# One kernel on one Trainium2 core: the first row tiles in one transfer, the first weights ahead of the filter's second piece, and 200 places of the order list

## Chip, core and metric

One NeuronCore of a Trainium2 chip runs the whole program. The metric is the device time of one execution in microseconds (us). Three runs of the kernel before gave 195.13, 194.25 and 196.08 us; the median, 195.13, is the time before.

## What is computed

The input `x` (2048 rows of 512, bf16) is normalized row by row. Two branches use the result `xn`: a state-space branch (a short convolution of `k`, times `v`, then a long convolution along the rows with a filter `ssm_k`, times `xn`), and a gated feed-forward branch (512 to 1792 to 512). Cut to what matters:

```python
xn = layernorm(x)                                   # x = A_q
kv = shift_conv(k, shift_k, taps=4) * v
y  = irfft(rfft(kv, 2S) * rfft(ssm_k, 2S))[:S]      # long convolution, S = 2048
s  = xn * (y + kv * ssm_D)
g  = silu((gelu(xn @ w_gate) * (xn @ w_up)) @ w_down)
out = x + s * g
```

## The kernel before, in words

**Tiling.** Row `16p + t` of `x` is partition `p` of row tile `t`, so 16 row tiles of 128x512. The feed-forward branch takes them in four groups `q` of four. In a group, each of 14 units `m` multiplies the transposed `xn` by a block of `Wg` and of `Wu` (four matmuls each, line 618 is the helper that records every plain matmul), ACT applies Gelu into `GE`, DVE multiplies into `HT`; then the `down` matmuls with `Wd` follow.

**The filter.** `ssm_k` comes as four pieces of 128x2048 into `Hn`. Pieces 0 and 1 are transposed on PE (`h_transpose`, lines 870 to 888, the matmuls of L878) into `HTr`; pieces 2 and 3 are rearranged on ACT into `HP` and transposed by DMA into `HTD`. A first Fourier step on PE with the table `F1` then makes eight tiles `AH0` to `AH7` from `HTr` ("H" tiles) and eight, `AJ0` to `AJ7`, from `HTD` ("J" tiles), in `stage1_h` (line 929). Each is evicted from PSUM into one of four places in SBUF and stored from there to the DRAM scratch `ZH`: an H tile by a DMA that ACT issues, a J tile by one that SP issues. `AH4` to `AH7` are made in two halves (`half1`, line 919, rows `X<-psall 128x4x128`), one for each filter piece, so such a tile holds its place from the first half until its store has landed.

**Places that are shared.** The four places of the H tiles are parts of `X` that are not loaded yet, and two of the four places of the J tiles are the same memory (line 485):

```python
ast = {"H": [quarter(X, j) for j in (8, 10, 12, 14)],
       "J": [quarter(T, j) for T, j in ((X, 12), (X, 14), (G, 4), (G, 6))], ...}
```

So J place 0 is H place 2, and J place 1 is H place 3. Each place has a semaphore that its stores raise, `d_astH0` to `d_astH3` and `d_astJ0` to `d_astJ3`. The recorder (`Trk.op`, line 195) makes an instruction wait for the stores of exactly the memory that it overwrites.

**What sets the order.** A planner (`Sched.run`, line 345) walks the list of task numbers `SEQ` in its written order and hands each task to its engine, so `SEQ` alone sets the order of each engine's instructions. From costs in a table the planner also works out times for every task; these decide nothing but which buffer or PSUM bank a tile gets (`Pool_.find`, line 250: the place that came free first; of places free equally long, the first). A tile gets its place when the list comes to the first eviction that writes it. For the first loads the planner is told when they land (`LANDS`, line 304).

**Start.** SP issues the loads one after the other (`load`, line 594, all recorded at L590). PE multiplies zeros 11 times to pass the time (`warm_up`, from the tile `AST`), then transposes filter piece 0, and so on as the list says. DVE takes the statistics of each row tile (L821, L822), POOL the reciprocal root (L831, L832), DVE writes `XN` (L835), PE transposes it (L854), and ACT or DVE evicts it to `xnT` (L609, L612).

Of the kernel before, what the change touches and what calls it, by code (L numbers as in the profile page):

```python
# [22 lines left out]
LAST = [(0, 384), (384, 512)]  # L23
TURN = 8192
N_WARM = 11
ORDER = "x02 h0 h1 x22 w0 w1 h2 h3 D0 w2 s0 k0 v0 x1 w3 k1 v1 d0 d1 k2 v2 k3 v3 x2 x3"
SEQ = (
# [22 lines left out]
)  # L50
NF_BANKS = 4
ISSUE = 470.0
LOAD_NS = {("x0_", 262144): 1400.0, ("x0_", 131072): 450.0, 262144: 900.0, 524288: 1350.0, ("x", 524288): 2100.0, ("h", 524288): 1300.0, ("wg", 524288): 1550.0, ("wu", 524288): 1450.0, 917504: 2620.0, ("sk", 524288): 1500.0, 344064: 1250.0, 46080: 350.0, 3072: 100.0, 1024: 200.0}
W_XT, W_SW, W_BK, W_BH, W_ZI, W_BI, W_ZK, W_MI, W_G1 = 1665000, 600000, 555000, 703000, 333000, 640000, 490000, 740000, 222000
NC_PAIRS = 4
SMALL = 1.15 * 262144
# [235 lines left out]
class Sched:  # L292
# [8 lines left out]
    FIRST = {"loads": 1050.0, "SP": 30500.0}  # L301
    DRAIN = 121.0
    EARLY, TAKEN, SHARED, WAIT = (0.0, 1.0), 1400.0, 46000.0, 3300.0
    LANDS = (4350.0, 5590.0, 7100.0, 8420.0, 9350.0, 10200.0, 11500.0)

    def __init__(self):
        self.tasks = []
# [37 lines left out]
    def run(self):  # L345
        free = dict(self.FIRST)
        pipe = 0.0
        n_loads = 0
        order = []
        pmode = 0  # L350
        for name in SEQ.split():
            t = self.tasks[int(name.rstrip("b"))]
            eng, dur = t.opts[name[-1] == "b"]
            base = 0.0
            for d in t.deps:
                base = max(base, d.end if eng == d.eng == "PE" else d.end + d.lat + (self.SEM if not d.nbytes or eng != "PE" else 400.0 if d.eng == "loads" else self.HEDGE))
            for b in t.w:
                if b.pool is not None and b.slot is None:
                    f, b.slot = b.pool.find()
                    b.pool.take(b.slot)  # L360
                    base = max(base, f + self.SEM)
            t.start, t.eng = max(base, free.get(eng, 800.0)), eng
            free[eng] = t.end = t.start + dur + (self.DRAIN if eng == "PE" and t.mode != pmode else 0.0)
            pmode = t.mode if eng == "PE" else pmode
            if eng == "loads":
                free[eng] = t.start + dur * (self.EARLY[1] if t.start < self.EARLY[0] else 1.0)
                if n_loads < len(self.LANDS):
                    free[eng] = self.LANDS[n_loads] - self.LOAD_LAT
                n_loads += 1
                t.end = free[eng] + self.LOAD_LAT  # L370
            elif t.nbytes:
                en = t.end
                if en < self.SHARED:
                    free["loads"] += self.TAKEN
                pipe = max(pipe, en + self.DMA_LAT / 2) + t.nbytes / (self.SHARE_BW if en < self.SHARED else self.DMA_BW)
                t.end = pipe + self.DMA_LAT / 2 + (self.WAIT if en < self.SHARED else 0.0)
            for b in set(t.r + t.w):
                b.left -= 1
                b.last_end = max(b.last_end, t.end + t.lat)
                if b.left == 0 and b.pool is not None:  # L380
                    b.pool.release(b.slot, b.last_end)
            order.append(t)
        assert sorted(t.n for t in order) == list(range(len(self.tasks)))
        return order
# [14 lines left out]
def build_kernel(nc, A_q, A_k, A_v, A_shift_k, A_ssm_k, A_ssm_D, B_w_gate, B_w_up, B_w_down, out):  # L399
    with ExitStack() as es0:  # L400
# [107 lines left out]
        def dsem(name):  # L508
            return DSem(nc.alloc_semaphore(name), name)
# [79 lines left out]
        def dma(eng, out_ap, in_ap, sem, r, w):  # L589
            trk.dma(eng, lambda e: e.dma_start(out=out_ap, in_=in_ap), sem, r=r, w=w)  # L590
# [3 lines left out]
        def load(name, out_ap, in_ap, w_res, w_buf, nbytes, ring="SP", r=(), rb=()):  # L594
            sem = dsem("d_" + name)
            ns = LOAD_NS.get((name.rstrip("0123456789"), nbytes)) or LOAD_NS[nbytes]
            last_load[0] = S.add([("loads", ns)], lambda e: dma(ring, out_ap, in_ap, sem, r, w_res), r=rb, w=w_buf, nbytes=nbytes)
# [211 lines left out]

        for what in ORDER.split():  # L810
            if what[0] in "xa" and len(what) == 3:
# [475 lines left out]
```

## Time and profile before

| | |
|---|---|
| Runs | 195.13, 194.25, 196.08 us |
| Span of the profiled execution (first to last instruction) | 193.3 us |
| Median of the runs minus that span | 1.8 us |
| Busy: PE, DVE, ACT, POOL | 188.6, 160.0, 125.4, 13.9 us |
| Mean granted TensorE clock | 1.00 |
| DMA | 49.19 MB, mean 254 GB/s |

The profiled execution is one of its own; its span leaves out what lies ahead of the first instruction and behind the last. Sums in the prediction are made in the time of that span, and the 1.8 us are added at the end. In the views a row names line, engine, operation, `out<-in` and a count; in square brackets stands the idle time of the engine just before, and what ended it. "SPq" and "ACTq" are the issues of DMAs. Matmul rows overlap: a 128x512 matmul has a duration of 379 ns in the views, while the next one starts 216 ns after it.

### The profile page before, as it was taken

What the parts mean: (1) busy time and instruction counts of PE and PEld (TensorE: products, weight loads), DVE (VectorE), ACT (ScalarE), POOL (GpSimd) and SP (SyncE); (2) the same over time, 40 slices, a digit from 0 to 9 for tenths busy, and PEclk for the clock granted to TensorE, in tenths of its full rate; (3) what the DMA queues carried; (4) which work ended last, traced back from release to release, by engine and by line L of the source; (5) the groups of instructions that cost most, each with busy time, mean ns of one, the idle gap of its engine ahead of it and who ended that gap; (6) DMA issues with size and microseconds to landing.
All of it is one profiled execution on the core that took longest, in us unless ns stands there. A gap on an engine that the chain in (4) does not pass through costs nothing.

```text
span 193.3 us, 3502 instructions
## 1 busy us (share of the span) xinstructions
PE 188.6 (98%) x1377; PEld 85.6 (44%) x1377; DVE 160.0 (83%) x245; ACT 125.4 (65%) x170; POOL 13.9 (7%) x32
## 2 busy tenths in 40 slices
PE   7899999999999999999999999999999999999993
PEld 2685544444444444443434433433444334444452
DVE  6699789998999995877888789878897863588993
ACT  6787999969885987868548766856577431232121
POOL 5412420000000000020300000000000000000000
PEclk9999999999999999999999999999999999999999
DMA  5999999999999679999999991984805345939333
GB/s 175 311 307 349 377 400 347 157 249 372 375 374 354 196 264 259 390 323 305 218 285 230 338 320 59 288 276 147 264 10 195 106 140 153 389 112 353 132 139 136
DMA packets 45958, 49.19 MB, mean 254 GB/s; under 512 B 12787, under 2 KB 39671, under 8 KB 45942
## 3 DMA queue, kind: packets, MB, share of 16 engines
q1 hardware_dynamic: 37366, 42.67, 70.1%
q10 hardware_dynamic: 8576, 6.29, 10.3%
q8 instruction: 11, 0.18, 0.4%
q14 instruction: 5, 0.04, 0.1%
HBM read 27.39 MB, written 14.68 MB: 218 GB/s over the span
## 4 chain that ended last, share of the span: by engine, by line
PE 93%; DMA 4%; SPq 1%; DVE 1%; ACT 0%; issue 0%
PE psall L618 86%; PE psall L1028 5%; DMA Hn<-in_A_ssm_k_dram 4%; PE psall L854 1%; SPq L590 1%; PE psall L878 1%; DVE G L1175 0%; DVE G L1174 0%; ACT G L1172 0%
## 5 line engine op out<-in xcount | busy, mean ns | idle before, releaser
L618 PE MATMUL psall<-xnT,Wu 128*128 128x512 bf16 (+1 forms) x232 | 55.8, 372 | 0.0
L618 PE MATMUL psall<-xnT,Wg 128*128 128x512 bf16 (+1 forms) x232 | 55.3, 372 | 0.0
L618 PE MATMUL psall<-Wd,HT 128*128 128x512 bf16 (+2 forms) x238 | 52.0, 367 | 0.0
L1140 DVE TENSOR_TENSOR HT<-psall,GE 128x512 bf16<-128x512 f32 x54 | 36.7, 685 | 15.8 <-PE psall L618 15.4
L1137 ACT ACTIVATE GE<-psall 128x512 bf16<-128x512 f32 x54 | 31.7, 601 | 13.1 <-PE psall L618 12.9
L618 PEld LDWEIGHTS psall<-Wd,HT 128*128 128x128 bf16 x238 | 22.4, 98 | 25.9 <-issue 1.1
L618 PEld LDWEIGHTS psall<-xnT,Wg 128*128 128x128 bf16 x232 | 21.9, 98 | 25.4 <-issue 1.3
L618 PEld LDWEIGHTS psall<-xnT,Wu 128*128 128x128 bf16 x232 | 21.6, 98 | 25.9 <-issue 3.5
L609 ACT ACTIVATE X<-psall 128x1024 bf16<-128x1024 f32 (+1 forms) x18 | 15.1, 843 | 3.3 <-DMA ZH<-X 1.9
L609 ACT ACTIVATE HS<-psall 128x1024 bf16<-128x1024 f32 x14 | 13.7, 1022 | 4.4 <-PE psall L1028 4.4
L1164 ACT ACTIVATE G<-psall 128x512 bf16<-128x512 f32 x12 | 7.0, 598 | 12.9 <-PE psall L618 12.4
L1011 DVE TENSOR_TENSOR KAC<-KAC,KTM 128x2048 bf16<-128x2048 bf16 x12 | 14.6, 1217 | 0.1
L1009 DVE TENSOR_TENSOR KTM<-KK,SKB 128x2048 bf16<-128x2048 bf16 x12 | 14.6, 1217 | 0.0
L609 ACT ACTIVATE BO<-psall 128x1024 bf16<-128x1024 f32 x9 | 9.1, 1022 | 8.2 <-PE psall L1028 7.7
L609 ACT ACTIVATE KB<-psall 128x1024 bf16<-128x1024 f32 x11 | 11.0, 1021 | 3.6 <-PE psall L1028 3.6
L609 ACT ACTIVATE AST<-psall 128x1024 bf16<-128x1024 f32 x12 | 12.4, 1033 | 0.7 <-PE psall L618 0.5
L612 DVE CAST BO<-psall 128x1024 bf16<-128x1024 f32 x7 | 8.5, 1224 | 3.7 <-PE psall L1028 3.7
L821 DVE BATCH_NORM_STATS2 stats<-X 128x6 f32<-128x512 bf16 x16 | 10.3, 675 | 1.1 <-DMA X<-in_A_q_dram 1.1
L1172 ACT ACTIVATE G<-psall 128x512 bf16<-128x512 f32 (+2 forms) x5 | 2.6, 512 | 13.1 <-PE psall L618 13.1
L1091 DVE TENSOR_TENSOR HW<-KB,HW 128x1024 bf16<-128x1024 bf16 x16 | 10.9, 682 | 0.0
L1091 DVE TENSOR_TENSOR HS<-KB,HS 128x1024 bf16<-128x1024 bf16 x16 | 10.8, 682 | 0.0
L1166 DVE SCALAR_TENSOR_TENSOR G<-G,psall 128x512 bf16<-128x512 bf16 x12 | 7.8, 680 | 2.0 <-ACT G L1164 2.0
(83 smaller groups left out, 175.6 us busy)
## 6 DMA issues: line engine op xcount, KB each, us to landing
BH<-ZH SPq DMA_DIRECT2D x8, 512.0 KB, 6.1
HW<-HS SPq DMA_DIRECT2D x16, 256.0 KB, 3.2
BK<-ZK SPq DMA_DIRECT2D x8, 512.0 KB, 5.1
ZI<-BO ACTq DMA_DIRECT2D x16, 256.0 KB, 2.8
BI<-ZI SPq DMA_DIRECT2D x8, 512.0 KB, 4.2
ZK<-AST SPq DMA_DIRECT2D x6, 512.0 KB, 4.1
Hn<-in_A_ssm_k_dram SPq DMA_DIRECT2D x4, 512.0 KB, 8.4
KK<-in_A_k_dram SPq DMA_DIRECT2D x4, 512.0 KB, 8.6
```

The lines of the kernel that those rows point to most:

```text
L609: return h.activation(o, i, ACTF.Copy, scale=scale)
L612: return h.tensor_copy(o, i)
L618: return h.matmul(o, lhsT=l, rhs=r, start=st, stop=sp)
L821: t_stats[t] = op([("DVE", 670.0)], lambda e, h, t=t: h.bn_stats(stats[:, t, :], X[:, t, :]), r=[bX[q][t % 4]], w=[bst[t]], rr=[R_X[t]], w ...
L1009: op([("DVE", dur)], lambda e, h, j=j, m=m: h.tensor_tensor(KTM[:, m.slot, :, :], kk(j), sk(j), ALU.mult), r=need + [bSKB[j], a], w=[m], r ...
L1011: op([("DVE", dur)], lambda e, h, m=m: h.tensor_tensor(KAC[:, a.slot, :, :], KAC[:, a.slot, :, :], KTM[:, m.slot, :, :], ALU.add), r=[m], ...
L1028: trk.op("PE", lambda h: h.matmul(ps(s, i)[b, :], lhsT=wt(col)[a, :], rhs=data(col)[a, :], start=n < 16, stop=n >= len(todo) - 16, tile_po ...
L1091: return hd.tensor_tensor(o, flat(KB, kb[h]), o, ALU.mult)
L1137: op([("ACT", act(512))], lambda e, h: h.activation(GE[:, g.slot, :], bank(pg), ACTF.Gelu_apprx_tanh), r=[pg], w=[g], rr=lambda: R_bank(pg ...
L1140: op([("DVE", dve(512, 1))], lambda e, h: h.tensor_tensor(HT[:, q % 2, m, :], bank(pu), GE[:, g.slot, :], ALU.mult), r=[pu, g], w=[bHT[q][m]],
L1164: op([("ACT", act(n))], lambda e, h, g=g, pc=pc: h.activation(g, pc(), ACTF.Tanh, scale=0.5), r=[p], w=[bt], rr=lambda p=p: R_bank(p), ww= ...
L1166: op([("DVE", dve(512, 1))], lambda e, h, g=g, pc=pc: h.scalar_tensor_tensor(out=g, in0=g, scalar=1.0, in1=pc(), op0=ALU.add, op1=ALU.mult ...
```

## The change

It has three parts. Row tiles 0 to 3 come in one transfer of 512 KB in place of two of 256 KB (`x04` for `x02` and `x22` in `ORDER`); there is one load task less, so every later task has a number lower by one. The first blocks of `Wg` and `Wu` (`w0`, in the list their loads) are issued ahead of filter piece 1 (`h1`). And the first 200 or so places of `SEQ` are written anew; behind them the two lists agree but for the numbers. `LANDS` is now given by bytes loaded and not by load. The diff, with `SEQ` cut to the rows that are rewritten:

```diff
-ORDER = "x02 h0 h1 x22 w0 w1 h2 h3 D0 w2 s0 k0 v0 x1 w3 k1 v1 d0 d1 k2 v2 k3 v3 x2 x3"
+ORDER = "x04 h0 w0 h1 w1 h2 h3 D0 w2 s0 k0 v0 x1 w3 k1 v1 d0 d1 k2 v2 k3 v3 x2 x3"
 SEQ = (
-    "17 18 0 3 1 2 4 8 5 7 11 20 6 9 50 12 65 66 67 73 19 68 75 74 49 10 76 13 52 21 82 22 86 117 83 69 107 70 71 112 54 72 87 77 56b 78 53 369 "
-    "51 108 36 79 371 109 84 88 80 370 15 85 372 23 31 89 110 378 377 113 27 373 379 381 383 375 14 453 455 457 380 24 458 374 459 25 454 118 382 "
-    "119 55 456 460 32 120 376 389 102 384 397 399 28 30 33 461 34 29 37 63 38 111 385 387 393 16 59 463 386 103 462 388 464 391 398 104 26 400 "
-    "390 395 105 465 146 394 405 396 99 147 121 466 148 468 150 407 57 409 100 401 403 46 392 402 406 149 151 470 35 404 152 39 96 413 408 469 "
-    "410 472 153 467 411 101 415 473 412 421 154 414 416 58 471 155 422 417 61 423 424 106 429 156 97 114 158 93 60 62 431 44 425 426 427 428 115 "
+    "0 17 18 1 3 8 2 19 20 21 4 11 12 5 6 7 35 9 10 13 66 22 30 26 49 23 24 64 31 67 27 51 74 68 48 65 72 69 75 82 86 76 50 70 106 111 29 101 73 "
+    "81 116 102 71 78 77 83 53 107 85b 376 378 79 14 52 84 88b 87 458 377 369 452 379 456 112 380 382 368 370 371 117 453 55 32 459 372 374 15 "
+    "388 381 454 383 455 33 54 62 373 28 375 384 457 390 392 394 36 37 113 103 393 104 105 386 16 25 45 118 56 119 389 391 396 460 464 461 398 "
+    "145 412 400 395 462 108 148 147 465 114 385 146 149 109 397 110 463 469 58 402 466 387 404 399 413 420 414 470 408 422 150 415 410 405 467 "
+    "34 151 152 153 98 99 57 421 423 120 401 403 38 409 411 60 471 468 472 100 59 61 406 154 155 407 424 426 43 428 157 95 416 417 430 425 427 "
...
-LOAD_NS = {("x0_", 262144): 1400.0, ...
+LOAD_NS = {("x0_", 524288): 1400.0, ...
-    LANDS = (4350.0, 5590.0, 7100.0, 8420.0, 9350.0, 10200.0, 11500.0)
+    LANDS = ((0.0, 2650.0), (524288.0, 4050.0), (1048576.0, 5450.0), (1310720.0, 6320.0), (1572864.0, 7190.0), (2097152.0, 8590.0), (2621440.0, 10590.0), (3145728.0, 12390.0))
...
-                if n_loads < len(self.LANDS):
-                    free[eng] = self.LANDS[n_loads] - self.LOAD_LAT
-                n_loads += 1
+                n_loads += t.nbytes
+                for (b0, t0), (b1, t1) in zip(self.LANDS, self.LANDS[1:]):
+                    if b0 < n_loads <= b1:
+                        free[eng] = t0 + (t1 - t0) * (n_loads - b0) / (b1 - b0) - self.LOAD_LAT
```

Line numbers above 300 are higher by two in the changed kernel: L618 is L620 there, L609 is L611.

**The order at three places.** SP's first issues, before:

```order
L590 DMA X<-in_A_q_dram 128x1024
L590 DMA Hn<-in_A_ssm_k_dram 128x2048
L590 DMA X<-in_A_q_dram 128x1024
L590 DMA Hn<-in_A_ssm_k_dram 128x2048
L590 DMA Wg<-in_B_w_gate_dram 128x4x256
L590 DMA Wu<-in_B_w_up_dram 128x4x256
L590 DMA X<-in_A_q_dram 128x2048
```

and now (the last row is the load of row tiles 4 to 7 in both):

```order
L592 DMA X<-in_A_q_dram 128x2048
L592 DMA Hn<-in_A_ssm_k_dram 128x2048
L592 DMA Wg<-in_B_w_gate_dram 128x4x256
L592 DMA Wu<-in_B_w_up_dram 128x4x256
L592 DMA Hn<-in_A_ssm_k_dram 128x2048
L592 DMA X<-in_A_q_dram 128x2048
```

The second piece of the filter moved from the fourth place to the fifth, and 2.0 MB in place of 1.5 MB have been asked for when it has.

PE after the multiplications by zero, up to the second piece of the filter, with the semaphores that a row waits for (`d_h0` and `d_h1` are the landings of the filter's pieces, `d_wg0` that of the first block of `Wg`). Before:

```order
L878 MATMUL psall<-ident_63,Hn 128x128 [waits d_h0,s_POOL]
L878 MATMUL psall<-ident_63,Hn 128x128 x7
L854 MATMUL psall<-ident,XN 128x128 [waits s_DVE]
L854 MATMUL psall<-ident,XN 128x128 x3
L618 MATMUL psall<-HTr,F_58 128x256 [waits s_ACT]
L618 MATMUL psall<-HTr,F_58 128x256
L854 MATMUL psall<-ident,XN 128x128 [waits s_DVE]
L854 MATMUL psall<-ident,XN 128x128 x3
L618 MATMUL psall<-HTr,F_58 128x256 x4
L878 MATMUL psall<-ident_63,Hn 128x128 [waits d_h1]
```

and now:

```order
L880 MATMUL psall<-ident_63,Hn 128x128 [waits d_h0,s_POOL]
L880 MATMUL psall<-ident_63,Hn 128x128 x7
L856 MATMUL psall<-ident,XN 128x128 [waits s_DVE]
L856 MATMUL psall<-ident,XN 128x128 x3
L620 MATMUL psall<-HTr,F_58 128x256 [waits s_ACT]
L620 MATMUL psall<-HTr,F_58 128x256 x5
L856 MATMUL psall<-ident,XN 128x128 [waits s_DVE]
L856 MATMUL psall<-ident,XN 128x128 x3
L620 MATMUL psall<-HTr,F_58 128x256 x2
L856 MATMUL psall<-ident,XN 128x128 [waits s_DVE]
L856 MATMUL psall<-ident,XN 128x128 x3
L880 MATMUL psall<-ident_63,Hn 128x128 [waits d_h1,s_ACT]
```

Two more matmuls of the Fourier step and the transposes of a third row tile stand ahead of the second piece.

ACT from the last four H tiles to the first two J tiles. Rows `X<-psall 128x1024` evict a whole tile, first H tiles, then (behind the last `DMA ZH`) J tiles; `DMA ZH<-X` is the store of an H tile, and the last such row is the eighth store. Rows in between are left out. Before:

```order
L609 ACTIVATE X<-psall 128x1024 [waits d_astH0,s_PE]
...
L609 ACTIVATE X<-psall 128x1024 [waits d_astH2]
...
L609 ACTIVATE X<-psall 128x1024 [waits d_astH0]
L1137 ACTIVATE GE<-psall 128x512 [waits s_DVE,s_PE]
L609 ACTIVATE X<-psall 128x1024 [waits d_astH3,s_PE]
L590 DMA ZH<-X 128x4x256 [waits s_ACT] x2
...
L590 DMA ZH<-X 128x4x256
...
L609 ACTIVATE X<-psall 128x1024 [waits d_astH2,s_PE]
L609 ACTIVATE X<-psall 128x1024 [waits d_astH3,s_PE]
```

and now:

```order
L611 ACTIVATE X<-psall 128x1024 [waits d_astH0,s_PE]
...
L611 ACTIVATE X<-psall 128x1024 [waits d_astH1,s_PE]
...
L611 ACTIVATE X<-psall 128x1024 [waits d_astH3,s_PE]
L1139 ACTIVATE GE<-psall 128x512 [waits s_DVE]
L611 ACTIVATE X<-psall 128x1024 [waits d_astH0,s_PE]
L592 DMA ZH<-X 128x4x256 [waits s_ACT] x2
...
L592 DMA ZH<-X 128x4x256
...
L611 ACTIVATE X<-psall 128x1024 [waits d_astH2,s_PE]
L611 ACTIVATE X<-psall 128x1024 [waits d_astH3,s_PE]
```

The four whole H tiles reuse places 0, 2, 0 and 3 before, and 0, 1, 3 and 0 now. The last two rows, the first J tiles, name the same semaphores in both.

More of the change, by code (lines that the diff above doesn't have):

```diff
@@ L52 @@
 ISSUE = 470.0
-LOAD_NS = {("x0_", 262144): 1400.0, ("x0_", 131072): 450.0, 262144: 900.0, 524288: 1350.0, ("x", 524288): 2100.0, ("h", 524288): 1300.0, ("wg", 524288): 1550.0, ("wu", 524288): 1450.0, 917504: 2620.0, ("sk", 524288): 1500.0, 344064: 1250.0, 46080: 350.0, 3072: 100.0, 1024: 200.0}
+LOAD_NS = {("x0_", 524288): 1400.0, ("x0_", 131072): 450.0, 262144: 900.0, 524288: 1350.0, ("x", 524288): 2100.0, ("h", 524288): 1300.0, ("wg", 524288): 1550.0, ("wu", 524288): 1450.0, 917504: 2620.0, ("sk", 524288): 1500.0, 344064: 1250.0, 46080: 350.0, 3072: 100.0, 1024: 200.0}
 W_XT, W_SW, W_BK, W_BH, W_ZI, W_BI, W_ZK, W_MI, W_G1 = 1665000, 600000, 555000, 703000, 333000, 640000, 490000, 740000, 222000
@@ L347, in run @@
         pipe = 0.0
-        n_loads = 0
+        n_loads = 0.0
         order = []
```

35 rows, old and new, of the table SEQ are left out of this document.

## Prediction

> **What bounds the kernel now.** I read the page first, then the stretches, then what PE waits for, and last the start and the stretch around 50 us.
>
> ```profile
> span 193.3 us, 3502 instructions
> PE 188.6 (98%) x1377; PEld 85.6 (44%) x1377; DVE 160.0 (83%) x245; ACT 125.4 (65%) x170; POOL 13.9 (7%) x32
> PE 93%; DMA 4%; SPq 1%; DVE 1%; ACT 0%; issue 0%
> ```
>
> PE is busy 98% of the span and is 93% of the chain that ended last (third row). A mean of 98% can hide where the other 2% lie, so the span is cut:
>
> ```profile
> core 0: us, PE busy (x) PEld busy (x) DVE busy (x) ACT busy (x) POOL busy (x), PEclk, DMA share, GB/s
> 0.97:5.64 4.67, 4.67 (x12) 1.65 (x12) 3.92 (x16) 3.43 (x5) 3.10 (x11) 1.00 0.78 221
> 5.64:11.23 5.59, 4.87 (x37) 3.90 (x37) 3.69 (x10) 3.79 (x6) 2.61 (x7) 1.00 1.00 339
> 11.23:80.00 68.77, 68.77 (x355) 33.52 (x356) 63.18 (x82) 59.33 (x81) 4.70 (x6) 1.00 1.00 315
> 80.00:160.00 80.00, 80.00 (x824) 32.11 (x823) 65.90 (x105) 51.78 (x69) 3.19 (x4) 1.00 0.74 224
> 160.00:190.00 30.00, 30.00 (x153) 14.25 (x152) 22.02 (x31) 6.49 (x10) 0.00 (x0) 1.00 0.59 210
> ```
>
> From 11.23 to 190 PE has no idle time at all; between 5.64 and 11.23 it has 5.59 - 4.87 = 0.72 us. The waits of PE between 5.6 and 193 us, and one row of those of ACT between 20 and 60 us (total, times, longest):
>
> ```profile
> PE psall L878 <- DMA Hn<-in_A_ssm_k_dram: 0.5, 1, 0.5
> PE psall L618 <- ACT HTr L609: 0.2, 1, 0.2
> ```
>
> ```profile
> ACT X L609 <- DMA ZH<-X: 1.9, 2, 1.0
> ```
>
> So the start can give back at most the 0.72 us, and nothing else on PE can be won, since the matmuls stay the same ones. What can be lost is larger: any new wait on PE behind 11.23 goes into the end one for one. The ACT row says that evictions into `X` already wait, twice, for a store of the memory they overwrite; so far PE does not feel it.
>
> **The start.** PE's rows there:
>
> ```profile
> 5.64 1.71 PE L878 MATMUL psall<-ident,Hn 128*128 128x128 f32 x8
> 7.82 0.39 PE L618 MATMUL psall<-HTr,F 128*128 128x256 bf16 x2 [0.25 <-ACT HTr L609]
> 8.04 0.39 PE L854 MATMUL psall<-ident,XN 128*128 128x128 bf16 x4
> 8.27 0.60 PE L618 MATMUL psall<-HTr,F 128*128 128x256 bf16 x4
> 9.32 1.16 PE L878 MATMUL psall<-ident,Hn 128*128 128x128 f32 x8 [0.46 <-DMA Hn<-in_A_ssm_k_dram]
> ...
> 14.96 1.02 PE L618 MATMUL psall<-xnT,Wg 128*128 128x512 bf16 x4
> ```
>
> The loads: two rows of the chain (start, us), two of SP's timeline, and the rows of the same two loads in the DMA view, whose last number is the time from issue to landing.
>
> ```profile
> 1.64 0.43 SPq L590
> 2.12 7.16 DMA Hn<-in_A_ssm_k_dram
> ```
>
> ```profile
> 3.08 0.70 SPq L590 DMA_DIRECT2D Wu<-in_B_w_up_dram  x1
> ...
> 4.42 0.64 SPq L590 DMA_DIRECT2D Wg<-in_B_w_gate_dram  x1
> ```
>
> ```profile
> Wu<-in_B_w_up_dram SPq DMA_DIRECT2D x1, 256.0 KB, 7.9
> Wg<-in_B_w_gate_dram SPq DMA_DIRECT2D x1, 512.0 KB, 10.4
> ```
>
> The filter's second piece, the last of 1.5 MB, lands at 2.12 + 7.16 = 9.28, and PE goes on 0.04 later. With the change it is the last of 2.0 MB. The load that ends 2.0 MB now is `Wu`: 3.08 + 7.9 = 10.98. The DMA engines are full there (share 1.00), so bytes decide, and the piece lands between 9.28 and 10.98. Three things follow:
>
> - Work put ahead of the piece: two 128x256 matmuls and four transposes. Four transposes take 8.27 - 8.04 = 0.23 us; a 128x256 matmul half of a 128x512 one, so 0.11 each: 0.45 us together.
> - The 0.25 us before `HTr` stay: the same 12 instructions stand ahead of that wait. They lie ahead of the piece's landing, which sets what follows.
> - The piece at the middle, 10.13, is 0.85 later than now: 0.85 - 0.45 = +0.4 us. At 10.98 it is 1.70 - 0.45 = +1.25; if it came so early that all idle time went, -0.7.
>
> Next comes the second block of `Wg`. It lands at 4.42 + 10.4 = 14.82 and is used at 14.96, just behind. In the new order ten 128x256 matmuls (eight with `Wu`, two with `HTr`) that stood ahead of that use stand behind it: PE wants the block 10 x 0.11 = 1.1 us earlier in its work. The bytes ahead of it are the same 3.0 MB, and one issue fewer (2.12 - 1.64 = 0.48 us) stands ahead on SP. If it lands at 14.82, PE's schedule moves by 14.86 + 1.1 - 14.96 = +1.0; if the saved issue brings it to 14.34, by +0.5. The wait that costs more counts, so I take **+0.5 us for the start**, with ends -0.7 and +1.25. Merging the row tiles costs and gives nothing beyond this: DVE's statistics begin behind the 11 multiplications by zero anyway.
>
> **The place that is shared.** This decides. Places go out in the order in which the list first writes them. Before, the halves `AH5`, `AH6`, `AH7`, `AH4` come in that order and get places 0, 1, 2, 3; now they come 4, 5, 6, 7, so `AH6` gets place 2 and not 1. `AH6`'s store is the eighth and last of ACT in both orders, because its second half is. The first J tile's place is the same memory as place 2. ACT's timeline:
>
> ```profile
> 36.14 0.41 ACTq L590 DMA_DIRECT2D ZH<-X  x1
> ...
> 40.27 0.42 ACTq L590 DMA_DIRECT2D ZH<-X  x1
> ...
> 45.04 0.37 ACTq L590 DMA_DIRECT2D ZH<-X  x1
> ...
> 49.15 1.02 ACT L609 ACTIVATE X<-psall 128x1024 bf16<-128x1024 f32 x1
> ```
>
> The row at 49.15 is the first J tile's eviction; it has no idle time in brackets, for the store it waits for, place 2's, was issued at 36.14 and has long landed. With the change it waits for the store issued at 45.04. How long stores take, from the DMA view of the issues at 36.14, 39.16, 40.27 and 45.04, and the longest of the eight:
>
> ```profile
> ZH<-X ACTq DMA_DIRECT2D x1, 256.0 KB, 4.2
> ZH<-X ACTq DMA_DIRECT2D x1, 256.0 KB, 4.8
> ZH<-X ACTq DMA_DIRECT2D x1, 256.0 KB, 7.8
> ZH<-X ACTq DMA_DIRECT2D x1, 256.0 KB, 7.2
> ZH<-X ACTq DMA_DIRECT2D x1, 256.0 KB, 9.3
> ```
>
> The slow two travel with loads that SP issues just before:
>
> ```profile
> 40.39 0.48 SPq L590 DMA_DIRECT2D Wd<-in_B_w_down_dram  x1
> 40.91 1.51 SPq L590 DMA_DIRECT2D V<-in_A_v_dram  x1
> ```
>
> Those loads and their place in SP's list don't change, so I take the mean of 7.8 and 7.2, 7.5 us; ends 4.2 and 9.3. Now the wait on PE. It makes the J tiles in pairs of PSUM banks, and the third tile takes the first one's pair:
>
> ```profile
> 50.18 1.03 PE L618 MATMUL psall<-xnT,Wg 128*128 128x512 bf16 x4
> 51.04 0.59 PE L618 MATMUL psall<-HTD,F 128*128 128x512 bf16 x2
> ```
>
> The row at 51.04 is that third tile; PE gets there now without waiting, since the eviction ended at 50.17. An eviction of that size and its handover to PE:
>
> ```profile
> 6.74 1.02 ACT L609 ACTIVATE HTr<-psall 128x1024 bf16<-128x1024 bf16 x1 [1.19 <-PE psall L878]
> ```
>
> It ends at 7.76 and PE's waiting row starts at 7.82: 0.06. The handover from a landing was 0.04. So the sum:
>
> - last store issued 45.04 + 0.5 (PE's shift reaches ACT) = 45.54; landed 45.54 + 7.5 = 53.04
> - eviction 53.08 to 54.10, PE's third J tile at 54.16
> - against 51.04: **+3.1 us**, of which 0.5 is the start and 2.6 a new pause of PE.
>
> The start's shift is inside this sum and not added once more. Queued behind the waiting eviction on ACT are the second J tile's eviction and the Gelu activations of the running group; DVE's products and PE wait for those, but PE is stopped by the third J tile before it gets to them. Behind the pause the order and the work are the same as before, and PE has nothing idle there in which to catch up. Span 193.3 + 3.1 = 196.4; the median of the runs is 1.8 above the span, so **198.2 us**. The new start order of DVE, POOL and the evictions I cost at nothing: what they delay is covered by the pause, and without that cover it is in the -0.7 to +1.25.
>
> **The rivals.**
>
> *The store is home in time.* PE, shifted by 0.5, comes to the third J tile at 51.54; the eviction must end at 51.48, so the landing must be by 50.4, a transit of at most 4.9 us. For it: two of the eight took 4.2 and 4.8. Against it: both were issued before the `Wd` and `V` loads above, and the one that now carries this wait took 7.2. Then only the start counts: 195.13 + 0.5 = **195.6**, between 194.4 and 196.4. It is the way to no change or a small gain. Chance 0.16.
>
> *The store takes as long as the longest.* The start's shift may push the last three stores together under those loads. 45.54 + 9.3 = 54.84, and 1.12 on: 55.96, +4.9: **200.0**. Against it: the loads don't move. Chance 0.10.
>
> *The pause cools PE's clock.* The first rows of PE are slow:
>
> ```profile
> 0.97 4.87 PE L618 MATMUL psall<-AST 128*128 128x512 bf16 x11 [0.97 <-DVE AST L671]
> ```
>
> 4.87 / 11 = 0.44 us for what takes (51.04 - 50.18) / 4 = 0.215 later, and the eight transposes at 5.64 take 1.71 against 1.16 at 9.32, though the granted clock in the table above is 1.00. So from 0.97 to about 7.3 PE ran at half rate; if the new pause brings that back, up to 6.4 / 2 = 3.2 us more: **201.4**. No pause of this trace is above 0.5 us, so no row tells how long one must be. Chance 0.06.
>
> By the Trainium skill ("TensorE: Matmul & The Clock Gate", Part 1: The HAM clock gate) the clock falls after an idle window of about 3.4 us; by that rule a pause of 2.6 us leaves the clock up and adds nothing, and one of 4.4, as with the longest store, could add this rival's price. The half rate of the first rows agrees with the page's cold rate; the rest no row here shows.
>
> *The weights don't come earlier in effect.* All 16 DMA engines are full, so the filter's piece and the second block of `Wg` could land on the late ends, 10.98 and 14.82: the start loses 1.25, 0.75 more than summed, and the sum becomes +3.85: **199.0**. Chance 0.08.
>
> **How the numbers follow.** The forecast has 0.60, the four rivals 0.16, 0.10, 0.06 and 0.08. The forecast's own range, transit 6.5 to 8.3 with the same start, is 197.2 to 199.0, the fourth rival at its end. The whole range reaches down to the first rival and up past the second: 195.6 to 200.6. One per cent is 1.95 us, about what a measurement of this kernel can tell from no change: slower means above 197.08. That holds for all cases but the first rival (0.16) and a transit between 4.9 and 6.3 (some 0.05 of the forecast); faster would need a start better than the -0.7, 0.03. So faster 0.03, same 0.18, slower 0.79.
>
> **What would show it.** Right: in the changed profile an eviction into `X` on ACT at about 53 with some 3.4 us idle before it, released by the DMA `ZH<-X`; a pause of PE of about 2.6 us at the third J tile, released by that eviction; none other behind 15 us; the filter's second piece landing at 10 to 11. The start is wrong if PE's back-to-back stretch begins before its old place. All is wrong if PE shows no pause around 52, or if the store was issued well before 45 us.

## The result, and the profile after

The changed kernel takes 201.97 us (median of six runs, 200.04 to 202.47) against 194.6 us for the kernel before measured beside it: a ratio of 1.0364, 95% interval 1.0335 to 1.0393. (A ratio is worked out from the single executions and is not quite the quotient of the two medians.) That is slower, as forecast, but by 7.4 us and not by 3.1, and above the range. The profiled execution of the changed kernel has a span of 200.6 us, 7.3 more than the 193.3 of before, and these 7.3 us are what has to be found. Both profiled executions are somewhat long ones of their kernel: the six of the changed kernel have a median of 201.97 and this one took 202.38, and the 20 executions of the kernel before that were measured beside e5 to e8 have a median span of 192.75. So a span of an experiment, set against 193.3, looks about half a microsecond better than its ratio does. The ratios below leave out one execution each of e4 (200.28 us) and e10 (199.91 us), which were more than 1.5% above the fastest of their kernel. The page:

```profile
span 200.6 us, 3504 instructions
PE 191.3 (95%) x1377; PEld 85.5 (43%) x1377; DVE 161.1 (80%) x246; ACT 125.5 (63%) x169; POOL 15.0 (8%) x32
PEclk9999999999959999999999999999999999999999
PE psall L620 74%; PE psall L1030 5%; DMA ZH<-X 4%; DMA X<-in_A_q_dram 2%; ACT X L611 1%; ACT GE L1139 1%; ACT HP L611 1%; POOL mv L834 1%; ACT TFA L731 1%; PE psall L856 1%; DVE stats L823 1%; DVE KAC L1007 1%; DVE KTM L1011 1%; DVE HT L1142 1%; PE psall L880 0%
```

Two things are new. `DMA ZH<-X`, the store of an H tile, stands in the chain that ended last with 4%. And PE is busy for 191.3 us and not 188.6 with the same 1377 matmuls, while the row of the granted clock has one slice at 5 tenths: some matmuls took longer. The stretches between 30 and 80 us show where, PE's busy time being the second number and the clock the last but two:

```profile
30.00:45.00 15.00, 15.00 (x73) 6.54 (x72) 14.72 (x17) 14.01 (x18) 0.00 (x0) 1.00 0.92 227
45.00:60.00 15.00, 10.88 (x42) 4.38 (x40) 11.00 (x13) 8.66 (x12) 0.00 (x0) 0.81 1.10 344
60.00:80.00 20.00, 20.00 (x92) 8.89 (x90) 16.86 (x17) 15.07 (x20) 0.00 (x0) 0.97 0.70 195
```

PE lacks 4.1 us between 45 and 60. The second J tile before, then PE's timeline around the hole now, and ACT's:

```profile
49.75 0.59 PE L618 MATMUL psall<-HTD,F 128*128 128x512 bf16 x2
```

```profile
50.02 0.59 PE L620 MATMUL psall<-HTD,F 128*128 128x512 bf16 x2
50.45 1.03 PE L620 MATMUL psall<-xnT,Wg 128*128 128x512 bf16 x4
55.59 1.04 PE L620 MATMUL psall<-HTD,F 128*128 128x512 bf16 x2 [4.12 <-ACT X L611]
56.42 1.91 PE L620 MATMUL psall<-xnT,Wu 128*128 128x512 bf16 x4
...
60.69 0.84 PE L620 MATMUL psall<-V,F 128*128 128x512 bf16 x2
61.36 1.03 PE L620 MATMUL psall<-xnT,Wg 128*128 128x512 bf16 x4
```

```profile
45.42 0.37 ACTq L592 DMA_DIRECT2D ZH<-X  x1
...
48.92 0.60 ACT L1139 ACTIVATE GE<-psall 128x512 bf16<-128x512 f32 x1
54.52 1.94 ACT L611 ACTIVATE X<-psall 128x1024 bf16<-128x1024 f32 x2 [5.00 <-DMA ZH<-X]
```

The row at 55.59 is the third J tile, the one at 54.52 the first J tile's eviction (two evictions in one row). The eviction stood 5.0 us for the store issued at 45.42. The chain of waits says the same in three steps:

```profile
45.42 9.01 DMA ZH<-X
...
54.52 1.03 ACT X L611
...
55.59 1.46 PE psall L620 x3
```

Behind the pause the same four `Wu` matmuls take 1.91 us and not 1.03. Cut finer, the granted clock falls to half while PE stands, at about 54.35, and comes back at about 61.1:

```profile
54.00:54.50 0.50, 0.00 (x0) 0.00 (x0) 0.50 (x1) 0.00 (x0) 0.00 (x0) 0.84 0.59 75
...
55.60:57.00 1.40, 1.40 (x4) 0.58 (x5) 0.00 (x0) 1.19 (x2) 0.00 (x0) 0.50 1.08 370
...
60.00:61.00 1.00, 1.00 (x4) 0.30 (x2) 1.00 (x2) 0.32 (x2) 0.00 (x0) 0.50 1.03 324
61.00:62.00 1.00, 1.00 (x5) 0.42 (x4) 1.00 (x2) 0.97 (x2) 0.00 (x0) 0.92 2.29 159
```

So the 7.3 us come in three parts. The second J tile is made at 50.02 and not 49.75: **0.27** from the start. Without a wait the third would come at 51.04 + 0.27 = 51.31; it comes at 55.59: **4.28** of pause. From the third J tile to the last step of ACT in the chain, `ACT G`, 189.57 - 51.04 = 138.53 us went by before and 196.87 - 55.59 = 141.28 do now: **2.75** of half clock; from 55.59 to 61.1 thirteen matmuls start 0.427 us apart and not 0.216, which is 13 x 0.211 = 2.74. The two ends, before and now:

```profile
189.57 0.50 ACT G L1172
```

```profile
196.87 0.50 ACT G L1174
```

The sum of the prediction had 3.1 of these 7.3 us. Of the 4.2 that it lacks, 55.59 - 54.16 = 1.43 are there at the third J tile, and 2.75 are the clock.

The start itself looks different from what was summed. The first of the transposes of the filter's two pieces:

```profile
6.67 1.13 PE L880 MATMUL psall<-ident,Hn 128*128 128x128 f32 x8 [0.82 <-DMA Hn<-in_A_ssm_k_dram]
8.07 0.40 PE L856 MATMUL psall<-ident,XN 128*128 128x128 bf16 x4 [0.26 <-DVE XN L837]
...
10.11 0.68 PE L880 MATMUL psall<-ident,Hn 128*128 128x128 f32 x4
```

The filter's first piece (issued at 1.18, 5.4 us) lands at 6.54 in place of 5.37, since 512 KB lie ahead of it and not 256; PE comes to it 1.03 us later than before. DVE's statistics wait for the same 512 KB: the first begins at 5.22 and not at 4.01, and PE stands 0.26 us for the first `XN`. The second piece lands at 9.97, where the prediction had 10.13, and costs no wait.

### The profile page after: what moved, and what is told of

Same layout as the page of the kernel before. It is cut to its first block, busy times and chain, and to the rows that moved or that the text cites. A ratio compares the mean times of both kernels' runs of the same rounds, so it can differ in the third digit from the quotient of the medians.

```text
span 200.6 us, 3504 instructions
## 1 busy us (share of the span) xinstructions
PE 191.3 (95%) x1377; PEld 85.5 (43%) x1377; DVE 161.1 (80%) x246; ACT 125.5 (63%) x169; POOL 15.0 (8%) x32
## 4 chain that ended last, share of the span: by engine, by line
PE 80%; DMA 7%; ACT 5%; DVE 3%; issue 2%; POOL 1%; ACTq 0%
PE psall L620 74%; PE psall L1030 5%; DMA ZH<-X 4%; DMA X<-in_A_q_dram 2%; ACT X L611 1%; ACT GE L1139 1%; ACT HP L611 1%; POOL mv L834 1%; ACT TFA L731 1%; PE psall L856 1%; DVE stats L823 1%; DVE KAC L1007 1%; DVE KTM L1011 1%; DVE HT L1142 1%; PE psall L880 0%
## 5 line engine op out<-in xcount | busy, mean ns | idle before, releaser
L620 PE MATMUL psall<-xnT,Wu 128*128 128x512 bf16 (+1 forms) x232 | 56.7, 377 | 0.0
L620 PE MATMUL psall<-xnT,Wg 128*128 128x512 bf16 (+1 forms) x232 | 55.9, 376 | 0.0
L620 PE MATMUL psall<-Wd,HT 128*128 128x512 bf16 (+2 forms) x238 | 52.0, 367 | 0.0
L620 PEld LDWEIGHTS psall<-Wd,HT 128*128 128x128 bf16 x238 | 22.4, 98 | 25.9 <-issue 1.1
L620 PEld LDWEIGHTS psall<-xnT,Wg 128*128 128x128 bf16 x232 | 22.3, 99 | 26.0 <-issue 2.7
L620 PEld LDWEIGHTS psall<-xnT,Wu 128*128 128x128 bf16 x232 | 21.8, 99 | 26.6 <-issue 4.6
L611 ACT ACTIVATE X<-psall 128x1024 bf16<-128x1024 f32 (+1 forms) x18 | 14.6, 839 | 8.4 <-DMA ZH<-X 5.0
L611 ACT ACTIVATE HS<-psall 128x1024 bf16<-128x1024 f32 x14 | 13.7, 1022 | 4.4 <-PE psall L1030 4.4
L611 ACT ACTIVATE BO<-psall 128x1024 bf16<-128x1024 f32 x9 | 9.1, 1023 | 8.2 <-PE psall L1030 7.7
L611 ACT ACTIVATE KB<-psall 128x1024 bf16<-128x1024 f32 x11 | 11.0, 1021 | 3.6 <-PE psall L1030 3.6
L611 ACT ACTIVATE AST<-psall 128x1024 bf16<-128x1024 f32 x12 | 12.3, 1025 | 0.7 <-PE psall L620 0.5
L1093 DVE TENSOR_TENSOR HS<-KB,HS 128x1024 bf16<-128x1024 bf16 x16 | 10.8, 682 | 0.0
```

The lines of the kernel that those rows point to most:

```text
L611: return h.activation(o, i, ACTF.Copy, scale=scale)
L620: return h.matmul(o, lhsT=l, rhs=r, start=st, stop=sp)
L1093: return hd.tensor_tensor(o, flat(KB, kb[h]), o, ALU.mult)
```

## The experiments

Each ratio is to the kernel before on the same chip, with its 95% interval.

**e1: the other place.** In the changed kernel

```diff
-"H": [quarter(X, j) for j in (8, 10, 12, 14)]
+"H": [quarter(X, j) for j in (8, 12, 10, 14)]
```

> The changed kernel with the second and third place of the H tiles exchanged, so that AH6 lies in X[10:12] and not under the first J tile. The theory of the shared place: the first J eviction waits for nothing, PE has no pause around 51 us, the clock stays at 1.00, and only the start's shift of about +0.3 us is left: span 193.6, time about 0.3 us (0.2%) over the kernel before. The rival, that the new order or the new loads cost the time by themselves: still 199 us or more.

Measured 197.04 us, ratio 1.0129 (1.0105 to 1.0153), profiled span 195.4. The J tiles are made at 49.53, 50.82, 52.12 and 53.41, without a pause. Two of PE's waits:

```profile
PE psall L880 <- DMA Hn<-in_A_ssm_k_dram: 0.8, 1, 0.8
PE psall L620 <- ACT X L611: 0.7, 1, 0.7
```

Some 4.8 us of the 7.4 go with one exchange of two numbers: the shared place is the larger part. But 2.6 us stay where 0.3 were expected, so neither theory had it all. Two places show them. At the start the half rate lasts longer in this execution (the eight transposes at 6.68 take 1.94 us, and the six matmuls behind them):

```profile
6.68 1.94 PE L880 MATMUL psall<-ident,Hn 128*128 128x128 f32 x8 [0.84 <-DMA Hn<-in_A_ssm_k_dram]
...
8.89 1.46 PE L620 MATMUL psall<-HTr,F 128*128 128x256 bf16 x6
```

which makes the third J tile 52.12 - 51.04 = 1.08 us late. Most of that is this execution and not the change of places: with the same loads ahead and the same order of PE, the changed kernel, e3, e4, e7 and e10 make the second J tile at 50.01 to 50.03, e1 and e9 at 50.82 and 50.73, and only the latter two have the slow transposes. And at 61.6 PE waits 0.69 us for the fifth J tile's eviction, which needs place 0 again and so the first J tile's store. SP issues that at 53.77 here and at 51.21 before. In the changed kernel the large pause covers this. These two make 1.77 of the 2.1 us between the spans; the other 0.3, and the 0.5 by which the medians lie further apart than the spans, are not placed.

**e2: only the wait, in the kernel before.** The same diff in `before`, where `AH6` has place 1.

> The kernel before with the same exchange of the two places, which there puts AH6 under the first J tile: only the wait is added, order and loads stay. The theory: the store issued at 45.0 lands 7.2 us later at 52.3, PE goes on at 53.4 and not 51.0, a pause of 2.4 us and a span of 195.7; if a pause of that length does not cool the clock, +2.4 us (1.2%); if it does, 2.7 us more, +5.1 us. The rival, that the wait costs nothing without the new order: 193.3.

Measured 197.3 us, ratio 1.0162 (1.0111 to 1.0213), profiled span 194.7. PE's row and ACT's:

```profile
52.41 0.61 PE L618 MATMUL psall<-HTD,F 128*128 128x512 bf16 x2 [2.02 <-ACT X L609]
```

```profile
44.23 0.37 ACTq L590 DMA_DIRECT2D ZH<-X  x1
...
51.33 1.94 ACT L609 ACTIVATE X<-psall 128x1024 bf16<-128x1024 f32 x2 [2.90 <-DMA ZH<-X]
```

The store took 7.0 us and the pause is 2.0: the wait alone, without new loads and without a new list, behaves as the sum had it. (The span is 1.0 under the one expected because PE was 0.82 us earlier in this execution already at the second J tile, 48.93 and not 49.75; its full rate began at 3.7 us, during the multiplications by zero.) Of the four executions two are at 196.5 us with a mean clock of 1.00, and two at 198.1 and 198.4 with 0.99. That a pause of about this length cools the clock in some executions and not in others is the likely reading; the two slower ones were not traced.

**e3: the pause filled.** In the changed kernel the group of four `Wg` matmuls ahead of the third J tile is made five times.

```diff
-for kd in range(KD):
+for kd in list(range(KD)) * (5 if (q, m, nm) == (1, 10, "g") else 1):
```

> The changed kernel with the four Wg matmuls that stand ahead of the third J tile made five times over (each time from the start, so the same result): PE is busy for 3.45 us of the 4.1 us pause. The theory that the pause cools the clock: granted clock 1.00 after it, the wait for the store the same, and the 2.75 us behind the pause gone: span 197.9, 2.7 us under the changed kernel. The rival, that PE runs slowly there for another reason (the DMA traffic, the order): span 200.6 as before, or more.

Measured 199.65 us, ratio 1.0258 (1.0235 to 1.0282), span 197.2.

```profile
50.45 4.48 PE L620 MATMUL psall<-xnT,Wg 128*128 128x512 bf16 x20
54.92 0.61 PE L620 MATMUL psall<-HTD,F 128*128 128x512 bf16 x2
55.37 1.03 PE L620 MATMUL psall<-xnT,Wu 128*128 128x512 bf16 x4
```

```profile
45.00:60.00 15.00, 14.89 (x68) 6.67 (x69) 12.22 (x14) 10.50 (x16) 0.00 (x0) 1.00 1.10 346
```

PE does 3.5 us of work that nobody needs, and the kernel is 2.3 us faster. The matmuls behind run at full rate from the first on (1.03 us for four, against 1.91), and the clock is 1.00. All four executions show 1.00. The store landed 0.7 us earlier here, and the third J tile is made at 54.92 and not 55.59; from there to the last step of ACT go 138.55 us, which is the 138.53 of before, so the whole 2.75 is gone. That settles the third part: the pause had cooled the clock.

**e4: less load beside the store.** In the changed kernel the numbers 40 and 41, the two loads of `Wd`, are moved behind 44, a load of `k`.

> The changed kernel with both loads of Wd issued behind the next load of k, so that 1.8 MB less is under way when the last store of an H tile goes out. The theory that the loads make that store slow: a transit of 5 to 7 us in place of 9, landing at 50.5 to 52.5, a pause of 0.5 to 2 us, clock 1.00, span 194 to 196. The rival, that the three stores close behind one another in ACT's queue make it slow: still 9 us and a span of 200.

Measured 197.32 us, ratio 1.0141 (1.0121 to 1.0161), span 195.3. The last H store, issued at 45.31, in the DMA view, and PE's pause:

```profile
ZH<-X ACTq DMA_DIRECT2D x1, 256.0 KB, 6.6
```

```profile
53.03 0.60 PE L620 MATMUL psall<-HTD,F 128*128 128x512 bf16 x2 [1.55 <-ACT X L611]
```

9.0 us became 6.6 and the pause 4.1 became 1.55, as the theory of the loads has it. It is not all: the two stores ahead still took 8.6 and 8.3 us without the loads of `Wd` (9.2 and 10.8 in the changed kernel). One of the four executions is at 200.28 with a clock of 0.991, the others near 197.2.

**e5: row tiles in two transfers.** e1 with

```diff
-ORDER = "x04 h0 w0 h1 w1 ...
+ORDER = "x02 h0 x22 w0 h1 w1 ...
```

and the list's numbers from 19 on higher by one, with 19, the new load, put in ahead of those of the first weights.

> e1 (the changed kernel with the two places exchanged) with row tiles 0 to 3 in two transfers again, the second behind the filter's first piece; weights still ahead of the filter's second piece, the order of every engine that of e1. The theory that the start of e1 is slow because 512 KB lie ahead of the filter's first piece (it lands at 6.55 and not 5.37, PE idles 0.8 us behind its zeros, and the clock comes up late): the piece lands at about 5.4, no idle time there, full rate from 7 us on, span about 1 us under e1: 194.3. The rival, that the new order itself costs e1 its time: span as e1, 195.2.

Measured 196.09 us, ratio 1.0080 (1.0046 to 1.0114), span 194.2, 1.2 under e1.

```profile
5.69 1.13 PE L880 MATMUL psall<-ident,Hn 128*128 128x128 f32 x8
8.09 0.40 PE L856 MATMUL psall<-ident,XN 128*128 128x128 bf16 x4 [1.27 <-DVE XN L837]
```

The piece is back at 5.6 and the idle time ahead of it gone, as expected; but the time is lost again 1.3 us later, where PE waits for DVE, whose new order takes statistics of a later row tile first and stands 1.09 us for that tile's load, now the second transfer, which lands at 6.79. The third J tile is made at 51.50, and e7, with one transfer and transposes at full rate too, makes it at 51.31: as far as these two profiles show, the split brought nothing at the start by itself. What e5 gains on e1 in the profile is the transposes' rate and the wait at 61 us, which it does not have. The span came out as forecast, but not for the reason given.

**e6: one transfer, in the kernel before.** `ORDER` begins `x04 h0 h1 w0`, the number 20 is taken out and the higher ones are lowered by one; no engine's order changes.

> The kernel before with row tiles 0 to 3 in one transfer and nothing else: the order of all engines is that of before. The theory that this delays the filter's first piece: it lands at about 6.5, PE waits 0.8 to 1.1 us more at the start, span 0.8 to 1.1 us over before, up to 2 us if the clock comes up late too. The rival, that the later piece is made good at the second one, which lands with the same bytes ahead: no difference.

Measured 195.24 us (ten runs), ratio 1.0037 (1.0019 to 1.0055), span 193.2. The transposes begin late by the 1.0 us that were expected,

```profile
6.62 1.13 PE L878 MATMUL psall<-ident,Hn 128*128 128x128 f32 x8 [0.78 <-POOL mv L831]
```

(named is POOL, but the piece landed at 6.5) and most of it is made good: the second piece is transposed at 9.31 and before at 9.32. The rival was nearer: 0.6 us of loss by the medians, none between the two profiled executions.

**e7: more zeros.** e1 with

```diff
-N_WARM = 11
+N_WARM = 13
```

> e1 with 13 multiplications by zero in place of 11, so that PE stays busy until the filter's first piece lands at 6.55. The theory that the idle time ahead of that piece lets the clock come up a step later: full rate from about 7 us on in every run, span 0.5 to 1 us under e1. The rival, that the landing alone sets the start: no difference from e1.

Measured 196.65 us, ratio 1.0097 (1.0066 to 1.0127), span 194.9: 0.4 us under e1, with ranges that overlap (195.81 to 196.73 and 196.52 to 197.43). In the profiled execution the transposes run at full rate and the third J tile comes at 51.31:

```profile
0.97 4.73 PE L620 MATMUL psall<-AST 128*128 128x512 bf16 x13 [0.97 <-DVE AST L673]
6.73 1.14 PE L880 MATMUL psall<-ident,Hn 128*128 128x128 f32 x8 [1.03 <-DMA Hn<-in_A_ssm_k_dram]
```

But the edit did not do what it was for. The 13 multiplications took 4.73 us, less than the 4.87 of the 11 in the kernel before, because the full rate began during the ninth of them; PE then idled 1.03 us ahead of the piece, more than the 0.84 of e1. The ninth is there in e1 too, so the two that were added are not what brought the rate up, and the run leaves the theory untested.

**e8: the weights first, in the kernel before.** Only 19, the filter's second piece, is moved behind 22.

> The kernel before with the first blocks of Wg and Wu ahead of the filter's second piece and nothing else. The theory by bytes: the piece lands at 10.1 to 11.0 in place of 9.3, and with nothing put ahead of it PE waits 0.8 to 1.7 us longer: span 194 to 195. The rival, that the filter's second piece has slack: no difference.

Measured 195.85 us (nine runs), ratio 1.0060 (1.0043 to 1.0076), span 194.1.

```profile
10.13 1.16 PE L878 MATMUL psall<-ident,Hn 128*128 128x128 f32 x8 [1.18 <-DMA Hn<-in_A_ssm_k_dram]
```

The transposes come 0.81 us later than before and the third J tile 0.80: the piece comes as late as the theory by bytes has it, and with nothing put ahead of it the delay goes through.

**e9: the store third from the end.** In the changed kernel one number of the list is moved:

```diff
-... 90 498 94 473 ... 226 478 115
+... 90 498 115 94 473 ... 226 478
```

> The changed kernel with one number of the list moved: AH6's store (115) goes out as the sixth of the eight H stores and not as the last, with places and everything else as they are. The theory of the shared place: the store is issued at about 40 and lands at about 49, so the first J eviction hardly waits; the last H store, now place 0's, concerns no J tile, and the seventh, place 3's, lands at about 52 and holds the second J tile up by 0.5 to 1 us: no pause of 4 us, clock 1.00, span 194.5 to 196. The rival, that any order of these three stores makes the first J tile late: 199 or more.

Measured 196.48 us, ratio 1.0097 (1.0069 to 1.0125), span 194.8. `AH6`'s store goes out at 40.15 and lands at 48.87. No J tile up to the fourth waits (49.44, 50.73, 52.03, 53.32); the second tile's place, expected at 52, was free at 51.0. What is left is a start that is late by 0.99 and 0.40 us at 61.2, as in e1. This is the change with its cause taken away and everything else in place.

**e10: other J places first.** In the changed kernel

```diff
-"J": [quarter(T, j) for T, j in ((X, 12), (X, 14), (G, 4), (G, 6))]
+"J": [quarter(T, j) for T, j in ((G, 4), (G, 6), (X, 12), (X, 14))]
```

> The changed kernel with the J places written in another order, so that the first two J tiles go into G and only the third and fourth into the H places. The theory: the wait moves to the third J tile's eviction, which is wanted at 52.9 and gets its place at 54.5; ACT stands 1.6 us, no J tile behind it needs its PSUM banks soon, so PE pauses little: span 194.5 to 196.5, clock 1.00. The rival, that the pause only moves with the wait: span 197 or more.

Measured 197.18 us, ratio 1.0115 (1.0078 to 1.0152), span 195.4.

```profile
54.53 1.02 ACT L611 ACTIVATE X<-psall 128x1024 bf16<-128x1024 f32 x1 [2.85 <-DMA ZH<-X]
```

```profile
55.61 0.61 PE L620 MATMUL psall<-V,F 128*128 128x512 bf16 x2 [1.53 <-ACT X L611]
```

The wait moved to the third J tile and shrank. But PE still pauses 1.5 us: a matmul group with `V` waits for that eviction, which the expectation had overlooked.

**e11: e7 with `Wd` later.**

> e7 (places exchanged, 13 zeros) with both loads of Wd issued behind the next load of k. e7 still has a pause of 1.1 us at 61 us: the fifth J tile waits for the first J tile's store, which SP issues at 53.6 (51.2 in the kernel before) because the transposing DMA ahead of it holds SP for 7.7 us (5.7 before). The theory that the backlog of loads holds that DMA: SP is free by 47, the store goes out by 51, no pause at 61, span about 193.7, within 1 us of the kernel before. The rival, that the fifth J tile is late for another reason: 194.8 as e7.

Measured 197.21 us, ratio 1.0113 (1.0072 to 1.0155), span 196.0: a miss. SP:

```profile
45.38 1.46 SPq L1041 DMA_TRANSPOSE MI<-TFA  x1
...
47.60 2.59 SPq L592 DMA_DIRECT2D Wd<-in_B_w_down_dram  x2
50.24 2.95 SPq L592 DMA_DIRECT2D ZK<-AST  x1
53.23 0.70 SPq L592 DMA_DIRECT2D ZH<-X  x1
```

The transposing DMA no longer holds SP (1.46 us, 7.7 in e7), but the issues behind it do, and the first J store goes out at 53.23 all the same. The fifth J tile is then late by 1.5 us, and the third is made 0.8 us later than in e7 (52.10), of which 0.4 are a wait of PE for a block of `Wg` at 21 us. That the transposition is what holds SP has fallen. What sets the time of SP's issues there is open.

None of these is below the kernel before. The nearest in which more is changed than the loads are e5 (1.0080), e7 and e9 (both 1.0097).

## Why the prediction was wrong in size and right in its mechanism

**The bound.** "Any new wait on PE behind 11.23 goes into the end one for one" was right for the wait and too small for the end: the end moved by the wait and by the cooled clock. Where the clock stayed up behind a wait at the third J tile, the rest of the work took as long as before: 138.54 us in e2, 138.55 in e3 and 138.54 in e4, against 138.53.

**The shared place.** Right in every step: `AH6` in place 2, its store the last, the first J eviction behind it, PE stopped at the third J tile, none of it made good later. e1, e2, e9 and e10 show it from four sides: other place, only the wait, other order of stores, other tile.

**The transit, the first step that failed.** The sum took "the mean of 7.8 and 7.2, 7.5 us", on the ground that "those loads and their place in SP's list don't change". Their place in the list did not, but their times did: SP issues them 0.3 to 1.1 us earlier (the loads of `Wd` at 40.08 and 41.37, before at 40.39 and 42.46), and ACT issues the last four stores 0.4 to 2.1 us later. The last four H stores of the changed kernel, issued at 38.27, 40.10, 41.51 and 45.42:

```profile
ZH<-X ACTq DMA_DIRECT2D x1, 256.0 KB, 3.4
ZH<-X ACTq DMA_DIRECT2D x1, 256.0 KB, 9.2
ZH<-X ACTq DMA_DIRECT2D x1, 256.0 KB, 10.8
ZH<-X ACTq DMA_DIRECT2D x1, 256.0 KB, 9.0
```

Before, the sixth, issued at 39.16, took 4.8 us and was home at 43.97. Now it is issued 0.94 us later, takes 9.2 and lands at 49.29; the seventh lands at 52.31 instead of 48.05, and the last one behind them at 54.43 instead of 52.27. This is the rival with the longest store, with what looks like its mechanism ("push the last three stores together under those loads") and nearly its transit, 9.0 against 9.3. It had 0.10. That the loads of `Wd` are a part of it e4 shows (6.6 us without them); how much is due to the two stores ahead was not taken apart. The term measured 9.0 us, 1.5 more than taken, and the store was issued 0.12 earlier than summed.

**The clock, the second step and the larger.** The sum had nothing for it. The rival "the pause cools PE's clock" had 0.06 and a price of up to 3.2 us; it came true with 2.75. The mistake was to treat it as a rival beside the longer store: the two hang together. The prediction said that a pause of 4.4 us "could add this rival's price", and then counted 200.0 for the longest store alone. By its own rows the joint case was 55.96 - 51.04 = 4.9 and up to 3.2 more, 193.3 + 8.1 + 1.8 = 203.2, and it was in no chance and outside the range. The measured 202 lies between that and the forecast. e3 shows the clock's part by itself.

How long a pause it takes the trace shows for one execution: PE's last matmul ahead of it ended at 55.59 - 4.12 = 51.47, and the clock fell at about 54.35, after 2.9 us without a matmul. The other five executions of the changed kernel show a mean clock of 0.983 to 0.991 as well. The pauses of 1.5 to 2.0 us in the profiled executions of e2, e4 and e10 left the clock at 1.00, while two, one and one of the other executions of these kernels show 0.99; how long PE paused in those no trace shows. A mean of 0.99 does not prove a pause either: e1 and e9, whose traces have no wait of PE above 1.0 us, have one such execution each.

The Trainium skill ("TensorE: Matmul & The Clock Gate", Part 1: The HAM clock gate) gives an idle window of about 3.4 us as the condition for the clock to fall. The trace agrees that a pause of 4.1 us lets it fall, but shows the fall after 2.9 us; the measurement decides, and the pause of 2.6 us that the prediction reckoned with lay close to it.

**The start.** +0.5 was forecast, 0.27 measured, for other reasons. The second piece of the filter landed where it was put (9.97, forecast 10.13). The second block of `Wg` came earlier than thought (4.16 + 9.4 = 13.56) and is first used at 13.91, without a wait. Not seen at all was the first piece: "Merging the row tiles costs and gives nothing beyond this" was wrong, for 256 KB more ahead of `Hn` make it land 1.17 us later. The reason given, that DVE's statistics begin behind the multiplications by zero anyway, was misread: before, they begin at 4.01 and the multiplications end at 5.84. That this execution shows only 0.27 is luck: its transposes already ran at full rate, 1.13 us, and those of the profiled execution of the kernel before did not, 1.71 us, though e6 and e8, whose PE starts with the same instructions, show 1.13 too. Where they are slow, as in e1, the start costs 1.08. Alone in the kernel before, the parts cost 0.6 us (e6) and 1.2 us (e8) by their medians.

**The cover.** "The new start order of DVE, POOL and the evictions I cost at nothing" holds only beneath the pause: with it gone, e1 is 2.6 us behind, of which the profile shows 1.08 at the start, a part of it the execution's slow transposes, and 0.69 at the fifth J tile.

## What to carry to other kernels

When a list decides who gets which buffer, read a reordering as a new assignment of memory too: name the last transfer out of each shared place and the first write into it, before and after. A new pause of the engine that bounds the kernel has to be priced with its clock, and a long transfer and a cold clock belong in one case, because the one brings the other. A transfer's duration belongs to its place among the others: when its neighbours on the queue move by a microsecond, take the row of the neighbour that it will resemble.

## What the runs showed of the hardware that was not expected

Useless work in a pause can pay: twenty matmuls in place of four made the kernel 2.3 us faster, chiefly because the clock stayed at 1.00. In the pause of 4.1 us the clock fell after 2.9 us, and then it took 5.5 us of matmuls at 0.427 us each before it was back. At the start, the full rate can begin at very different times with the same instructions ahead: in the profiled executions at 3.7 us in e2 and at 7.1 us in the kernel before. The granted clock is shown as 1.00 all that time, so there the rate can be read only from the matmuls. And a store of 256 KB that left its queue 0.94 us later took 4.4 us longer (4.8 to 9.2): before it landed ahead of the load of `V` issued just ahead of it (43.97 and 44.76), now behind two loads (45.21 and 46.88, itself at 49.29). The load of `k` was issued 0.7 us behind that store before and is issued 1.0 us ahead of it now. In e4, where no load of `Wd` is under way, the same store still took 8.6 us, so `Wd` is not the reason. That it shares the DMA engines with the loads ahead of it is read from these landings, and not tested by itself.
